# Local and global attention with an MLP on one core: the weights' lower parts move to VectorE, the loads get one fixed order with one more place, and zero products are put ahead of some of TensorE's first work

## The chip, the cores and the metric

The kernel runs on one core of a Trainium2 chip. Five engines work side by side: TensorE (PE, matrix products; its weight loads are listed as PEld), VectorE (DVE), ScalarE (ACT), GpSimd (POOL) and SyncE (SP), whose queue issues nearly all transfers. The metric is the device time of one execution in microseconds (us).

## The reference

Eight batches with eight heads of 64 are computed. 32 global queries see all 544 keys (32 global and 512 local); 512 local queries see the 32 global keys and those local keys that are at most 32 positions away. The attention's output, 4352 rows of 512 numbers, goes through x @ w_in, SiLU and @ w_out with 2048 hidden units, all in float32.

```python
s_ll = np.where(np.abs(pos[:, None] - pos[None, :]) <= window, s_ll, -1e9)
s_l  = np.concatenate([scale * q_l @ k_g.T, s_ll], axis=-1)
x    = np.concatenate([softmax(s_g) @ v_all, softmax(s_l) @ v_all], axis=2)
h    = x @ w_in
out  = (h * (1 / (1 + np.exp(-h)))) @ w_out
```

## The kernel before

**Stages and tiles.** Local attention is cut into stages: one for each batch b, each 128 local queries c and each pair of heads pr, 128 stages k in all. A stage is `st_load` (queries and keys, one DMA), `st_scores` (two products into a PSUM bank s; DVE adds the mask and takes the minimum in one instruction, L345; ACT takes the exponential, L349; DVE forms the reciprocals; ACT scales one half, L353, and DVE the other, L354), `st_turn` (four PE transposes by the identity, L382, copied back by ACT, L384) and `st_out` (eight small products with the values into a bank o, L413; ACT rounds them to xh, L420; DVE subtracts to get the rest xl, L421). Values are loaded by `st_vload`: one stage at a time for the first four, then four stages in one DMA. The global queries of a batch have four steps for pairs of heads: `g_load`, `g_scores` (L250, copied by ACT, L251), two softmaxes over 544 columns (`g_soft`, L270 to L275) and two groups of transposes (`g_turn`, L288 and L291). Global work of batch 0 lies among the first stages.

**The MLP.** Three output tiles of 128 rows (two at the end) make a block. For each block and each of 16 slices f of the hidden units, `first_layer` does 12 products of 384 columns (L568), ACT and DVE form the SiLU in two parts, gh (L577) and gl (L578), and `second_layer` adds three products for each tile (L590 to L592). All products use rounded numbers and the rest apart: high by high, high by rest, rest by high. After a product group `fill` calls `advance`, which emits the next attention steps, so attention for the next block is spread over the MLP of this one. Ahead of block 0 there is no MLP to spread it over: all twelve stages of that block stand there alone.

**The weights** arrive as 64-bit words. `fetch_weights` loads half a slice; `join_weights` makes float32 of it (ACT L203, DVE L205 and L206); `split_weights` rounds it with ACT (L215), and POOL subtracts the rounded part to get `w_lo` (L216). Six halves are joined and two slices split ahead of the MLP, the rest during its first block.

**What sets the order.** PE's order is the program's. Each step has a due time (`FIRST` for the first four stages, `DUE` and others later), all steps are sorted by it, and emitted in that order. On the other engines and on SP a planner that simulates the program chooses the order, except for instructions in `hold(...)`, which keep the program's order among themselves. The weights' instructions are held; the loads of stages from 28 on are held by `steady`; the first 28 stages' loads are left to the planner.

**Places.** `raw_tile` gives the early loads four places in turn: two of the pool `raws`, and two tiles that later hold rounded weights (`wh14`, `wh15`). A load into a place that is in use waits on SP for the products that read it, and every later load waits behind it. Early, banks of the MLP serve as extra banks for attention (`attbank`).

**At the start** POOL makes the identity, three masks, and clears the four whole tiles for probabilities, in an order that the planner chooses.

Of the kernel before, what the change touches and what calls it, by code (L numbers as in the profile page):

```python
# [9 lines left out]
F32 = mybir.dt.float32  # L10
F32R = mybir.dt.float32r
BF16 = mybir.dt.bfloat16
# [4 lines left out]
ALU = mybir.AluOpType  # L17
# [4 lines left out]
P = 128  # L22
NC = SL // P
NPR = H // 2
NST = NC * NPR
W = 224
# [15 lines left out]
KF = 24  # L42
GF = 3
KP = 12
SINGLE = 12
SCRATCH = 8
FETCH, LOOK = 6, 3
FIRSTW = {2: 1, 3: 1, 4: 1, 5: 1, 6: 1, 7: 1, 8: 1, 9: 1, 10: 1, 11: 1}
JOINS, SPLITS = (9.0, 9.6, 10.2, 10.8, 11.4, 12.0), (12.1, 12.7)

FIRST = dict(load=(-1.2, -1.1, -1.0, 0.1), vload=(-0.9, 0.2, 0.3, 1.1), turn=(3.2, 4.0, 4.9, 5.8), out=(4.3, 5.2, 6.1, 7.0),
             gload=(1.2, 2.2, 3.2, 3.3), gscores=(3.4, 4.2, 5.1, 6.0), gsoft=(4.4, 6.2), gturn=(6.9, 8.0),
             late=8.5, then=7.3)

DUE = dict(load=-1.2, split=-0.5, turn=1.6, out=2.2)
# [10 lines left out]
def attention_moe_kernel(ctx: ExitStack, tc: tile.TileContext, qk0_in, qk_in, v_in, gqk, wts, out):  # L66
# [25 lines left out]
        return ps_att.tile([P, 512], F32, tag=f"att{kind}", name=name)  # L92


    id32 = work.tile([P, P], F32R, tag="qk", bufs=BUFS["qk"], name="id32").bitcast(F32)
    make_identity(nc, id32)
    ident = const.tile([P, P], F32R, name="ident")
    nc.vector.tensor_copy(out=ident, in_=id32)

    masks = []  # L100
    for kind in range(3):
        m = const.tile([P, W], BF16, name=f"mask{kind}")
        nc.gpsimd.memset(m, 0.0)
        band = m[:, : W - SG]
        nc.gpsimd.affine_select(out=band, in_=band, pattern=[[1, W - SG]], compare_op=ALU.is_ge,
                                fill=NEG, base=0, channel_multiplier=-1)
        nc.gpsimd.affine_select(out=band, in_=band, pattern=[[-1, W - SG]], compare_op=ALU.is_ge,
                                fill=NEG, base=2 * HALO, channel_multiplier=1)
        if kind == 0:
            nc.gpsimd.memset(m[:, :HALO], NEG)  # L110
        if kind == 2:
            nc.gpsimd.memset(m[:, W - SG - HALO : W - SG], NEG)
        masks.append(m)
    mask_of = [masks[0]] + [masks[1]] * (NC - 2) + [masks[2]]


    taken = set()

    def scratch(i, dtype, name):
        return const.tile([P, 2 * DM], dtype, tag=f"wh{i}", name=name)  # L120
# [4 lines left out]
    probs += [more[:, DM * i : DM * (i + 1)].rearrange("p (u j) -> p u j", u=2) for i in range(2)]  # L125
    vfirst = scratch(7, F32, "vfirst")
    vsecond = scratch(5, F32, "vsecond")
    for t in probs:
        nc.gpsimd.memset(t, 0.0)
    pgs = [const.tile([P, SKV], F32, name=f"pg{i}") for i in range(2)]  # L130

    pts = [const.tile([P, 2, 2, P + SG], F32, name=f"pt{i}") for i in range(BUFS["pt"])]
# [16 lines left out]
    homes = itertools.count()  # L149

    def raw_tile(name, whole=False):
        i = next(homes) % 4 if whole else 0
        if i % 2 and 14 + i // 2 not in taken:
            return scratch(14 + i // 2, F32, name)
        return raws.tile([P, QW + KW], F32, tag="raw", name=name)
# [5 lines left out]


    w_32, w_hi, w_lo, w_raw, w_next = [], [], [], [], [0, 0]

    hold = tc.keep_in_program_order

    def steady(k, load):
        if k >= ND:
            hold(load)

    def fetch_weights():
        i = w_next[0]
# [36 lines left out]
    def split_weights(f):  # L209
        w_hi.append(const.tile([P, 2 * DM], F32R, tag=f"wh{f}", name=f"w_hi{f}"))  # L210
        w_lo.append(const.tile([P, 2 * DM], F32R, tag=f"ws{f}", name=f"w_lo{f}"))
        for c0 in range(0, 2 * DM, DM):
            sl = slice(c0, c0 + DM)
            hi, lo, w = w_hi[f][:, sl], w_lo[f][:, sl], w_32[2 * f + c0 // DM]
            hold(nc.scalar.copy(out=hi, in_=w))  # L215
            hold(nc.gpsimd.tensor_tensor(out=lo, in0=w, in1=hi.bitcast(F32), op=ALU.subtract))  # L216


    state = {}

    def g_load(b, p):
        raw = raw_tile(f"raw_g{b}_{p}", b < GF)
        steady(b * NST - 4, nc.sync.dma_start(out=raw[:, :GW], in_=gqk[b, p]))
        state["graw", p] = raw

    def g_split(b, p):
# [50 lines left out]
    def g_turn(b, hh):  # L277
        did(("turn", b, hh), ("soft", b, hh), ("turn", b, 0) if hh else ("last", b - 1))
        if hh == 0:

            state["pgt"] = (work.tile([P, NC, H, SG], F32, tag="pgt", name=f"pgt{b}"),
                            work.tile([P, QG], F32, tag="pgu", name=f"pgu{b}"))
        pgt, pgu = state["pgt"]
        hs = slice(4 * hh, 4 * hh + 4)
        tb = attbank("t", f"gt{b}_{hh}")
        for i in range(4):
            sl = slice(i * P, (i + 1) * P)
            nc.tensor.transpose(tb[:, sl], pgs[hh][:, sl], ident.bitcast(F32))  # L288
        nc.scalar.copy(out=pgt[:, :, hs, :], in_=tb.rearrange("p (t h q) -> p t h q", t=4, h=4))
        tb = attbank("s", f"gu{b}_{hh}")  # L290
        nc.tensor.transpose(tb[:SG, :P], pgs[hh][:, 4 * P :], ident.bitcast(F32))  # L291
        for i in range(2):
            rows, src = slice(SG * (2 * hh + i), SG * (2 * hh + i + 1)), tb[:SG, QG * i : QG * (i + 1)]
            nc.scalar.copy(out=pgu[rows, :], in_=src)
# [4 lines left out]
    def st_load(k, b, c, pr):  # L299
        raw = raw_tile(f"raw{k}", k < ND)  # L300
        if k < ND:
            nc.sync.dma_start(out=raw[:, : QW + W], in_=qk0_in[k])
        else:
            steady(k, nc.sync.dma_start(out=raw, in_=qk_in[k - ND]))
        tiles["raw", k] = raw

    def st_vload(k, b, c, pr):
        n = NPR - pr if k >= NPR else 1
        if k < 2 * NPR:
            vraw = (vfirst, vsecond)[k // NPR][:, VW * pr : VW * (pr + n)]  # L310
        else:
            vraw = raws.tile([P, NPR * VW], F32, tag="vraw", bufs=1, name=f"vraw{k}")
        vraw = vraw.rearrange("p (n w) -> p n w", n=n)
        steady(k, nc.sync.dma_start(out=vraw, in_=v_in[b, c, pr : pr + n].rearrange("n p w -> p n w")))
        for i in range(n):
            tiles["vraw", k + i] = vraw[:, i].rearrange("p (a u d) -> p a u d", a=2, u=2)

# [10 lines left out]
    def st_scores(k, b, c, pr):  # L328
        if k < ND:
            raw = tiles.pop(("raw", k))  # L330
        else:
            qk, klo = tiles.pop(("qk", k))
        s = attbank("s", f"s{k}")
        ss = [s[:, u * W : (u + 1) * W] for u in range(2)]
        for u in range(2):
            qs, ks = slice(u * P, (u + 1) * P), slice(u * W, (u + 1) * W)
            if k < ND:
                nc.tensor.matmul(ss[u], raw[:, qs], raw[:, QW : QW + W], start=True, stop=True)
            else:
                nc.tensor.matmul(ss[u], qk[:, qs], qk[:, QW:][:, ks], start=True, stop=False)  # L340
                nc.tensor.matmul(ss[u], qk[:, qs], klo[:, ks], start=False, stop=True)  # L341
        p = probs_tile(k)
        st = small.tile([P, 8], F32, tag="st", name=f"st{k}")
        for u in range(2):
            nc.vector.tensor_tensor_reduce(out=p[:, u, :W], in0=ss[u], in1=mask_of[c],  # L345
                                           scale=-SCALE, scalar=3.0e38, op0=ALU.add, op1=ALU.min,
                                           accum_out=st[:, u : u + 1])
        for u in range(2):
            nc.scalar.activation(p[:, u, :W], p[:, u, :W], AF.Exp, bias=st[:, u : u + 1], scale=-1.0,  # L349
                                 accum_out=st[:, 2 + u : 3 + u])  # L350
        nc.vector.tensor_scalar(out=st[:, 4:6], in0=st[:, 2:4], scalar1=1e-9, scalar2=None, op0=ALU.add)
        nc.vector.reciprocal(out=st[:, 6:8], in_=st[:, 4:6])  # L352
        nc.scalar.activation(p[:, 0, :W], p[:, 0, :W], AF.Copy, scale=st[:, 6:7])  # L353
        nc.vector.tensor_scalar(out=p[:, 1, :W], in0=p[:, 1, :W], scalar1=st[:, 7:8], scalar2=None,  # L354
                                op0=ALU.mult)
        tiles["p", k] = p.rearrange("p u j -> p (u j)")
# [39 lines left out]
    def st_out(k0, n, b, c, t):  # L396
# [5 lines left out]
        for j in range(n):  # L402
            k = k0 + j
            vraw, pt = tiles.pop(("vraw", k)), tiles.pop(("pt", k))
            if k < NPR:
                tiles["late", k] = vraw
            if j % 2 == 0:
                banks_.append(attbank("o", f"o{k}"))
            o = banks_[-1][:, wide * (j % 2) : wide * (j % 2 + 1)]
            for a in range(2):  # L410
                m = wide if (a == 0 or c == NC - 1) and k >= NPR else P
                for u in range(2):
                    nc.tensor.matmul(o[D * u : D * (u + 1), :m], vraw[:, a, u, :], pt[:, u, a, :m], start=(a == 0),  # L413
                                     stop=(a == 1))
# [279 lines left out]
```

## Time and profile before

| | |
|---|---|
| median of 3 runs (lowest to highest) | 1004.57 us (1003.56 to 1006.97) |
| the profiled execution | 1005.77 us, of which the span of instructions is 1004.0 |
| PE busy | 968.4 us (96%) |
| DVE, ACT, POOL busy | 619.7, 580.9, 225.6 us |
| mean granted clock of PE | 0.988 |
| moved by DMA | 151.03 MB |

Stretches are given in microseconds from the start of the span. In the view of stretches each engine has its busy time and, in brackets, its instructions; then come PE's granted clock (1.00 is full), the share of the 16 transfer engines' time that was busy, and GB/s. In the view in order of time a row has start, length, engine, line, operation, output <- input, and in square brackets the idle time of the engine before it with what ended it. In the groups a row ends in busy time and mean ns of one, then the idle time before them. A row of waits has the total, the count and the longest. Matmuls overlap, so the length of one is more than its distance to the next.

### The profile page before, as it was taken

To read this page: it belongs to the slowest core of one execution; us is meant where nothing else is said; L and a number is where in the kernel's file an instruction comes from. 1 tells how busy PE (TensorE), PEld (TensorE's weight loads), DVE (VectorE), ACT (ScalarE), POOL (GpSimd) and SP (SyncE) were. 2 spreads that over 40 slices of the span, in tenths; PEclk is the share of its full clock that TensorE was granted. 3 is DMA by queue.
4 is the path that set the end of the run, shared out by engine and by line. 5 is a ranking of instruction groups with operands and counts; after the bars stand their busy time and mean duration, and the time that the engine had idled before them with its cause. 6 is when DMAs were issued, how large, how long until landed. Compare 5 with 4: busy or idle time off the path is not lost.

```text
span 1004.0 us, 17484 instructions
## 1 busy us (share of the span) xinstructions
PE 968.4 (96%) x5792; PEld 854.7 (85%) x5792; DVE 619.7 (62%) x1861; ACT 580.9 (58%) x1491; POOL 225.6 (22%) x421
## 2 busy tenths in 40 slices
PE   6888899999899999999999999999999999999998
PEld 4567778889798989998899989998998989889896
DVE  3678885566577567755576666775677665553332
ACT  5787765566566656654466656665666655443332
POOL 2144433222122221211222121222222221211000
PEclk8899999999999999999999999999999999999999
DMA  8574544656666656645476466565666555333000
GB/s 295 189 254 146 153 129 140 165 135 167 197 158 172 176 161 178 160 118 138 106 193 178 119 194 188 163 176 142 176 179 185 139 151 165 106 100 84 2 22 22
DMA packets 175626, 151.03 MB, mean 150 GB/s; under 512 B 115888, under 2 KB 135856, under 8 KB 175536
## 3 DMA queue, kind: packets, MB, share of 16 engines
q1 hardware_dynamic: 171312, 142.31, 50.8%
q10 hardware_dynamic: 4224, 7.60, 2.1%
q8 instruction: 46, 0.75, 0.3%
q14 instruction: 44, 0.36, 0.1%
HBM read 86.44 MB, written 36.18 MB: 122 GB/s over the span
## 4 chain that ended last, share of the span: by engine, by line
PE 78%; DMA 2%; DVE 2%; issue 2%; ACT 1%; POOL 0%; SPq 0%; POOLq 0%; DVEq 0%; ACTq 0%
PE h L568 33%; PE out L592 11%; PE out L590 11%; PE out L591 11%; PE o L413 6%; PE s L340 2%; PE s L341 2%; DMA raw<-in_qk_dram 1%; DMA raw_g<-in_gqk_dram 1%; PE gt L288 1%; DMA away<-halves 0%; PE gs L254 0%; PE gs L253 0%; DVE gl L578 0%; DVE w L206 0%
## 5 line engine op out<-in xcount | busy, mean ns | idle before, releaser
L568 PE MATMUL h<-xh,w_lo 128*128 128x384 f32 (+1 forms) x768 | 252.2, 328 | 2.8 <-POOL w_lo L216 2.8
L568 PE MATMUL h<-xh,w_hi 128*128 128x384 f32 (+1 forms) x768 | 253.4, 330 | 0.7 <-ACT w_hi L215 0.7
L568 PE MATMUL h<-xl,w_hi 128*128 128x384 f32 (+1 forms) x768 | 251.4, 327 | 0.3 <-DVE xl L421 0.3
L364 POOL COPY halves<-probs 128x512 uint16<-128x512 uint16 x208 | 135.0, 674 | 437.9 <-DVE probs L354 203.1
L590 PE MATMUL out<-w_hi,gh 128*128 128x512 f32 x544 | 221.1, 406 | 5.6 <-ACT gh L577 5.5
L592 PE MATMUL out<-w_hi,gl 128*128 128x512 f32 x544 | 216.5, 398 | 5.5 <-DVE gl L578 5.2
L591 PE MATMUL out<-w_lo,gh 128*128 128x512 f32 x544 | 214.1, 394 | 0.0
L574 ACT ACTIVATE t<-h 128x384 f32<-128x384 f32 (+1 forms) x192 | 90.6, 472 | 178.7 <-PE h L568 160.2
L575 DVE SCALAR_TENSOR_TENSOR t<-t,h 128x384 f32<-128x384 f32 (+1 forms) x192 | 101.7, 530 | 108.6 <-ACT t L574 107.5
L349 ACT ACTIVATE probs<-probs,st 128x224 f32<-128x224 f32 x244 | 115.8, 475 | 64.8 <-DVE st L345 63.8
L568 PEld LDWEIGHTS h<-xh,w_hi 128*128 128x128 f32 x768 | 145.0, 189 | 8.7 <-ACT w_hi L215 1.5
L568 PEld LDWEIGHTS h<-xl,w_hi 128*128 128x128 f32 x768 | 145.0, 189 | 7.1 <-DVE xl L421 0.6
L568 PEld LDWEIGHTS h<-xh,w_lo 128*128 128x128 f32 x768 | 144.7, 188 | 3.7 <-POOL w_lo L216 3.7
L578 DVE TENSOR_TENSOR gl<-t,gh 128x384 fp32r<-128x384 f32 (+1 forms) x192 | 107.4, 559 | 57.7 <-PE out L592 43.8
L592 PEld LDWEIGHTS out<-w_hi,gl 128*128 128x128 f32 x544 | 102.4, 188 | 35.6 <-DVE gl L578 13.4
L577 ACT CAST gh<-t 128x384 fp32r<-128x384 f32 (+1 forms) x192 | 94.5, 492 | 58.6 <-DVE t L575 58.0
L345 DVE CUSTOM_DVE_ANT_0 probs<-s,mask 128x224 f32<-128x224 f32 x244 | 85.7, 387 | 68.0 <-PE s L341 54.0
L590 PEld LDWEIGHTS out<-w_hi,gh 128*128 128x128 f32 x544 | 102.8, 189 | 27.3 <-ACT gh L577 11.0
L591 PEld LDWEIGHTS out<-w_lo,gh 128*128 128x128 f32 x544 | 102.9, 189 | 12.8
L324 ACT CAST qk<-raw 128x704 fp32r<-128x704 f32 x100 | 77.6, 776 | 31.9 <-DMA raw<-in_qk_dram 24.4
L325 DVE TENSOR_TENSOR klo<-raw,qk 128x448 fp32r<-128x448 f32 x100 | 64.8, 648 | 41.3 <-ACT qk L324 39.7
L353 ACT ACTIVATE probs<-probs,st 128x224 f32<-128x224 f32 x122 | 58.7, 481 | 33.5 <-DVE st L352 30.3
(86 smaller groups left out, 1122.3 us busy)
## 6 DMA issues: line engine op xcount, KB each, us to landing
raw<-in_qk_dram SPq DMA_DIRECT2D x100, 352.0 KB, 3.4
away<-halves SPq DMA_DIRECT2D x104, 256.0 KB, 2.6
vraw<-in_v_dram SPq DMA_DIRECT2D x30, 512.0 KB, 4.6
raw_w<-in_wts_dram SPq DMA_DIRECT2D x24, 512.0 KB, 4.6
raw_g<-in_gqk_dram SPq DMA_DIRECT2D x32, 304.0 KB, 4.0
out_dram<-o ACTq DMA_DIRECT2D x28, 256.0 KB, 3.6
raw<-in_qk_dram SPq DMA_DIRECT2D x28, 240.0 KB, 2.8
raw_w<-in_wts_dram SPq DMA_DIRECT2D x16, 256.0 KB, 3.3
```

What stands on the lines that cost most here:

```text
L324: nc.scalar.copy(out=qk, in_=raw)
L345: nc.vector.tensor_tensor_reduce(out=p[:, u, :W], in0=ss[u], in1=mask_of[c], scale=-SCALE, scalar=3.0e38, op0=ALU.add, op1=ALU.min, accum_ ...
L349: nc.scalar.activation(p[:, u, :W], p[:, u, :W], AF.Exp, bias=st[:, u : u + 1], scale=-1.0, accum_out=st[:, 2 + u : 3 + u])
L364: nc.gpsimd.tensor_copy(out=halves[:, :, u], in_=p[:, 2 * P * u : 2 * P * (u + 1)].bitcast(U16).rearrange("p (j h) -> p h j", h=2))
L568: nc.tensor.matmul(h[:, :nt], wt, x[:, c, :nt], start=(i == 0), stop=(i == 3 * NCC - 1))
L574: nc.scalar.activation(t[:, :nt], h[:, :nt], AF.Tanh, scale=0.5)
L575: nc.vector.scalar_tensor_tensor(out=t[:, :nt], in0=t[:, :nt], scalar=1.0, in1=h[:, :nt], op0=ALU.add, op1=ALU.mult)
L577: nc.scalar.copy(out=gh[:, :nt], in_=t[:, :nt])
L578: nc.vector.tensor_tensor(out=gl[:, :nt], in0=t[:, :nt], in1=gh[:, :nt].bitcast(F32), op=ALU.subtract)
L590: nc.tensor.matmul(o, gh[:, sl], wh, start=(f == 0), stop=False)
L591: nc.tensor.matmul(o, gh[:, sl], wl, start=False, stop=False)
L592: nc.tensor.matmul(o, gl[:, sl], wh, start=False, stop=(f == NF - 1))
```

## The change

Five things are changed.

1. `split_weights` subtracts on VectorE instead of GpSimd.
2. All loads are held: `g_load`, `st_load` and `st_vload` keep the program's order on SP together with the weights. In `FIRST` the first value loads move from −0.9, 0.2, 0.3 and 1.1 to 1.22, 1.23, 2.22 and 2.23; the global loads move from 1.2, 2.2, 3.2 and 3.3 to 1.2, 1.21, 2.2 and 2.21. The ten early weight loads, one each with stages 2 to 11, go two each with stages 4 and 5 and one each with 6 to 11.
3. The fifth early load gets a place of its own (`wh13`); the ring of four goes on behind it.
4. Products of a zero tile (bf16, 288 columns) are issued on PE into columns that the next group overwrites: 14 ahead of the first scores, 8 ahead of the second group of global transposes of batch 0, and 3 ahead of each o of stages 4 to 11.
5. POOL's first work is held in a new order: the first mask, then only the pads of the probability tiles (32 columns of each half), then the identity, then the other masks.

```diff
+WARM = 288
+WARMS = (14, 8, 3)
-FIRSTW = {2: 1, 3: 1, 4: 1, 5: 1, 6: 1, 7: 1, 8: 1, 9: 1, 10: 1, 11: 1}
+FIRSTW = {4: 2, 5: 2, 6: 1, 7: 1, 8: 1, 9: 1, 10: 1, 11: 1}
-FIRST = dict(load=(-1.2, -1.1, -1.0, 0.1), vload=(-0.9, 0.2, 0.3, 1.1), turn=(3.2, 4.0, 4.9, 5.8), out=(4.3, 5.2, 6.1, 7.0),
-             gload=(1.2, 2.2, 3.2, 3.3), gscores=(3.4, 4.2, 5.1, 6.0), gsoft=(4.4, 6.2), gturn=(6.9, 8.0),
+FIRST = dict(load=(-1.2, -1.1, -1.0, 0.1), vload=(1.22, 1.23, 2.22, 2.23), turn=(3.2, 4.0, 4.9, 5.8), out=(4.3, 5.2, 6.1, 7.0),
+             gload=(1.2, 1.21, 2.2, 2.21), gscores=(3.4, 4.2, 5.1, 6.0), gsoft=(4.4, 6.2), gturn=(6.9, 8.0),
...
+    zeros = two.tile([P, WARM], BF16, tag="gl", bufs=1, name="zeros")
+    nc.vector.memset(zeros, 0.0)
+
+    def warm(bank, n):
+        for _ in range(n):
+            nc.tensor.matmul(bank[:, 512 - WARM :], zeros[:, :P], zeros, start=True, stop=True)
...
-    for t in probs:
-        nc.gpsimd.memset(t, 0.0)
+    def pads():
+        for t in probs:
+            hold(nc.gpsimd.memset(t[:, :, W:], 0.0))
...
-        i = next(homes) % 4 if whole else 0
+        i = next(homes) if whole else 0
+        if whole and i == NPR:
+            return scratch(13, F32, name)
+        i = (i - (i > NPR)) % 4
...
-    def steady(k, load):
-        if k >= ND:
-            hold(load)
...
-            hold(nc.gpsimd.tensor_tensor(out=lo, in0=w, in1=hi.bitcast(F32), op=ALU.subtract))
+            hold(nc.vector.tensor_tensor(out=lo, in0=w, in1=hi.bitcast(F32), op=ALU.subtract))
...
-        steady(b * NST - 4, nc.sync.dma_start(out=raw[:, :GW], in_=gqk[b, p]))
+        hold(nc.sync.dma_start(out=raw[:, :GW], in_=gqk[b, p]))
...
+        if b == 0 and hh:
+            warm(tb, WARMS[1])
...
-            nc.sync.dma_start(out=raw[:, : QW + W], in_=qk0_in[k])
+            hold(nc.sync.dma_start(out=raw[:, : QW + W], in_=qk0_in[k]))
...
-        steady(k, nc.sync.dma_start(out=vraw, in_=v_in[b, c, pr : pr + n].rearrange("n p w -> p n w")))
+        hold(nc.sync.dma_start(out=vraw, in_=v_in[b, c, pr : pr + n].rearrange("n p w -> p n w")))
...
+        if k == 0:
+            warm(s, WARMS[0])
...
+                if NPR <= k < SINGLE:
+                    warm(banks_[-1], WARMS[2])
```

More of the change, by code (lines that the diff above doesn't have):

```diff
@@ L92, in attbank @@
         return ps_att.tile([P, 512], F32, tag=f"att{kind}", name=name)
[L95 to L114, printed above, removed]
+    hold = tc.keep_in_program_order
+    zeros = two.tile([P, WARM], BF16, tag="gl", bufs=1, name="zeros")
[3 more added lines that the diff above has]
+            nc.tensor.matmul(bank[:, 512 - WARM :], zeros[:, :P], zeros, start=True, stop=True)
     taken = set()
@@ L127, in attention_moe_kernel @@
     vsecond = scratch(5, F32, "vsecond")
-    for t in probs:
-        nc.gpsimd.memset(t, 0.0)
+    def pads():
+        for t in probs:
+            hold(nc.gpsimd.memset(t[:, :, W:], 0.0))
+    masks = []
+    for kind in range(3):
+        m = const.tile([P, W], BF16, name=f"mask{kind}")
+        hold(nc.gpsimd.memset(m, 0.0))
+        band = m[:, : W - SG]
+        hold(nc.gpsimd.affine_select(out=band, in_=band, pattern=[[1, W - SG]], compare_op=ALU.is_ge,
+                                     fill=NEG, base=0, channel_multiplier=-1))
+        hold(nc.gpsimd.affine_select(out=band, in_=band, pattern=[[-1, W - SG]], compare_op=ALU.is_ge,
+                                     fill=NEG, base=2 * HALO, channel_multiplier=1))
+        if kind == 0:
+            hold(nc.gpsimd.memset(m[:, :HALO], NEG))
+            pads()
+            id32 = work.tile([P, P], F32R, tag="qk", bufs=BUFS["qk"], name="id32").bitcast(F32)
+            make_identity(nc, id32)
+            ident = const.tile([P, P], F32R, name="ident")
+            nc.vector.tensor_copy(out=ident, in_=id32)
+        if kind == 2:
+            hold(nc.gpsimd.memset(m[:, W - SG - HALO : W - SG], NEG))
+        masks.append(m)
+    mask_of = [masks[0]] + [masks[1]] * (NC - 2) + [masks[2]]
     pgs = [const.tile([P, SKV], F32, name=f"pg{i}") for i in range(2)]
@@ L163, in attention_moe_kernel @@
     w_32, w_hi, w_lo, w_raw, w_next = [], [], [], [], [0, 0]
-    hold = tc.keep_in_program_order
-    def steady(k, load):
-        if k >= ND:
-            hold(load)
     def fetch_weights():
@@ L301, in st_load @@
         if k < ND:
-            nc.sync.dma_start(out=raw[:, : QW + W], in_=qk0_in[k])
+            hold(nc.sync.dma_start(out=raw[:, : QW + W], in_=qk0_in[k]))
         else:
-            steady(k, nc.sync.dma_start(out=raw, in_=qk_in[k - ND]))
+            hold(nc.sync.dma_start(out=raw, in_=qk_in[k - ND]))
         tiles["raw", k] = raw
```

## The prediction

> **What bounds the kernel now.** I read the busy times by stretch first, cut where the work of TensorE (PE) changes: loads and first scores, the first global queries, the rest of attention ahead of the MLP, the first MLP pass, and everything after it.
>
> ```profile
> core 0: us, PE busy (x) PEld busy (x) DVE busy (x) ACT busy (x) POOL busy (x), PEclk, DMA share, GB/s
> 0.00:11.67 11.67, 7.75 (x28) 5.93 (x28) 5.16 (x29) 6.74 (x22) 5.55 (x25) 1.00 0.82 253
> 11.67:24.71 13.04, 9.36 (x57) 6.06 (x57) 3.16 (x10) 7.04 (x19) 0.00 (x0) 0.74 0.93 331
> 24.71:28.08 3.37, 1.60 (x12) 1.27 (x10) 2.14 (x11) 2.66 (x11) 0.80 (x4) 1.00 0.80 274
> 28.08:35.11 7.03, 7.03 (x39) 5.45 (x37) 2.66 (x13) 3.59 (x12) 0.98 (x5) 0.51 0.34 113
> 35.11:55.15 20.04, 16.56 (x122) 12.10 (x121) 15.54 (x68) 19.06 (x58) 5.09 (x11) 1.00 0.66 216
> 55.15:150.00 94.85, 84.51 (x459) 69.97 (x457) 78.80 (x193) 68.75 (x175) 38.97 (x36) 0.98 0.53 168
> 150.00:1004.00 854.00, 841.64 (x5087) 753.95 (x5085) 512.23 (x1538) 473.01 (x1201) 174.20 (x344) 1.00 0.52 143
> ```
>
> From 150 us on PE works 841.64 of 854.00 us at full clock. The loads of that stretch keep their order among the steps, all but the last few subtractions of weights lie before it, and there is no filler in it: I carry it over unchanged. Everything is decided in the first 150 us, and since PE sets the rest, a microsecond won there is a microsecond at the end. Each of the first six stretches has another limit. Next I read PE's instructions in order of time, for the waits in brackets.
>
> ```profile
> 3.36 5.38 PE L338 MATMUL s<-raw 128*128 128x224 f32 x16 [3.36 <-DMA raw<-in_qk_dram]
> ...
> 11.04 0.63 PE L382 MATMUL t<-ident,probs 128*128 128x128 f32 x4 [0.50 <-ACT probs L353]
> 13.57 0.90 PE L250 MATMUL gs<-raw_g 128*64 128x272 f32 x3 [1.90 <-DMA raw_g<-in_gqk_dram]
> ...
> 18.50 1.62 PE L250 MATMUL gs<-raw_g 128*64 128x272 f32 x3 [1.78 <-DMA raw_g<-in_gqk_dram]
> ...
> 24.72 1.02 PE L338 MATMUL s<-raw 128*128 128x224 f32 x4
> 27.50 0.63 PE L288 MATMUL gt<-ident,pg 128*128 128x128 f32 x4 [1.76 <-DVE st L351]
> ...
> 42.91 0.66 PE L382 MATMUL t<-ident,probs 128*128 128x128 f32 x4 [1.07 <-ACT probs L353]
> ```
>
> Between 11.67 and 24.71 PE stops twice for global queries that have not landed, and the clock falls. The loads in the order of SP's queue, and the landing times of the global queries, say why:
>
> ```profile
> 7.13 0.65 SPq L185 DMA_DIRECT2D raw_w<-in_wts_dram  x1
> 7.82 0.73 SPq L314 DMA_DIRECT2D vraw<-in_v_dram  x1
> 8.60 0.69 SPq L185 DMA_DIRECT2D raw_w<-in_wts_dram  x1
> 9.38 1.06 SPq L223 DMA_DIRECT2D raw_g<-in_gqk_dram  x2
> ```
>
> ```profile
> DMA to landing us min/median/max: 2.7/4.5/9.2
> ```
>
> The third global load is issued at 9.38 and used at 18.50: those 9.1 us are the maximum of 9.2. Ahead of it stand weights and values that nobody reads before o and the MLP; the transfer engines are 93% busy, so it is a queue and not a latency. The last limit is in the first MLP pass, 55.15 to 150, where PE is idle for 10.3 of 94.85 us. Its waits:
>
> ```profile
> PE out L590 <- ACT gh L577: 3.3, 4, 1.6
> PE out L592 <- DVE gl L578: 3.1, 3, 2.4
> PE h L568 <- POOL w_lo L216: 2.8, 3, 1.1
> ```
>
> **The loads.** Eight rows of SP's issues change places. The four small value loads leave their places among the first scores' loads, the global loads come right behind these, and the weights and the large values stand behind the stage loads for k=4 and 5. Ahead of the last global load there are then, by their shapes, four stage loads (128 x 480 f32, 240 KB each), three global ones (128 x 608, 304 KB) and two values (128 x 256, 128 KB), about 2.1 MB. Before, the stage loads, four values, two global loads, three weights, vsecond and vraw (128 x 1024, 512 KB each of the last five) made 4.6 MB. The extra place lets the first global load go without a wait. The second now waits on SP for the scores of stage 0 (free at about 6 us), and behind it stand the values of stages 0 and 1 and the other global loads; o of stage 0 would wait for them. With the median landing of 4.5 us they are there at 10 to 12 us, which is when PE reaches gs and o (gs at best at 11.67). So both DMA waits go. What is late next is ACT: its 7.04 us of work between 11.67 and 24.71. PE's own work there is 9.36, but a mean clock of 0.74 over 13.04 us is 6.8 us at half clock, of which 1.8 were the second wait; 5.0 busy us at half speed become 2.5, leaving 6.9. The stretch can thus fall from 13.04 to 7.0 and no lower. PE and ACT hand tiles to each other stage by stage and neither fills 7 of 7; I take 8.5, **a gain of 4.5**, with 2 (a new wait on ACT chains as long as half of the old ones) and 6 as ends. The weights start some 7 us later than now; their first reader is at 40.4 us, so that is hidden by about 25 us:
>
> ```profile
> L205 DVE TENSOR_SCALAR raw_w<-raw_w x40: 282/422/1526, 40.4 to 149.8; 128x512 uint32<-128x512 uint32 x24, 128x256 uint32<-128x256 uint32 x16
> L206 DVE SCALAR_TENSOR_TENSOR w<-w,raw_w x40: 411/693/1578, 41.6 to 151.3; 128x512 uint32<-128x512 uint32 x24, 128x256 uint32<-128x256 uint32 x16
> ```
>
> Without that cover each weight piece would cost 512 KB at 331 GB/s, 1.5 us.
>
> **The zero products.** No row shows a bf16 product. The nearest are fp32r products of 384 columns, which start 0.17 us apart at full clock:
>
> ```profile
> 56.01 0.33 PE L568 MATMUL h<-xl,w_hi 128*128 128x384 f32 x1
> 56.18 0.33 PE L568 MATMUL h<-xh,w_lo 128*128 128x384 f32 x1
> ```
>
> 288 columns are then 0.13 us, or 0.26 at half clock; as the lower end I take nothing at all (a filler that lies wholly in a wait). The first 14 take 3.6 us cold. They begin at about 1 us, when the zeros are written, and end near 4.7, so they hold up the first scores by 1.3 us (these start at 3.36 now). That is hidden: the first reduction waits for a mask until 5.74.
>
> ```profile
> 5.74 0.39 DVE L345 CUSTOM_DVE_ANT_0 probs<-s,mask 128x224 f32<-128x224 f32 x1 [3.94 <-POOL mask L110]
> ```
>
> The mask comes first in POOL's new order, so without the fillers DVE would start near 4.3 (3.36 and two cold products); with them at about 5.5. The 1.3 us are lost out of what the mask gives. In return the clock is up sooner: the scores run 581 ns each at first and 352 later, which the clock column (1.00) doesn't show there.
>
> ```profile
> L338 PE MATMUL s<-raw x4: 581/581/581, 5.8 to 6.9; 128*128 128x224 f32 x4
> L338 PE MATMUL s<-raw x4: 352/352/353, 7.8 to 8.4; 128*128 128x224 f32 x4
> ```
>
> Stage 3's scores end near 7.9 instead of 8.74, but ACT is the limit there; **0.3** for the start (−1.3 to +1.0). The eight at the second transpose of the global softmax, 1.0 us, lie in the wait of 1.76: nothing. What they are worth is the clock after it:
>
> ```profile
> 14.00:15.00 1.00, 1.00 (x10) 0.72 (x8) 0.00 (x0) 0.52 (x2) 0.00 (x0) 0.73 1.11 392
> ...
> 28.00:29.00 1.00, 1.00 (x6) 0.93 (x4) 0.03 (x1) 0.95 (x3) 0.12 (x1) 0.55 0.00 0
> ```
>
> Waits of 1.90 and 1.76 us were each followed by a half clock, the one of 1.07 at 42.91 was not (the clock of 35.11 to 55.15 is 1.00). A filled gap leaves less than 1 us. Then the stretch from 28.08, PE busy throughout at clock 0.51, falls from 7.03 to 3.5 us of PE, or 3.59 of ACT; with the hand-overs 4.5, **a gain of 2.5** (0 to 3.4). The Trainium skill ("TensorE: Matmul & The Clock Gate", Part 1) says the clock halves only after about one idle window of 3.4 us. This trace differs: no gap after the first loads reached 2 us. By that rule the gap of 1.76 would not have cooled and these 2.5 would not be there to win; the rows decide.
>
> The last 24, three ahead of each o of stages 4 to 11, are 3.1 us of PE in a region where ACT is busy 19.06 of 20.04 us and PE idles 3.5. They go into waits, or move the next tile by less than the wait that follows: **a loss of 0.5** (0 to 3.1). If ACT stopped being the limit the whole 3.1 would show.
>
> **The subtraction on VectorE.** First DVE and POOL by shape from 50 to 155 us, then two of DVE's shapes between 200 and 800, where POOL subtracts nothing:
>
> ```profile
> L206 DVE SCALAR_TENSOR_TENSOR w<-w,raw_w 128x512 uint32<-128x512 uint32 x20 | 15.6, 778 | 4.1 <-ACT w L203 3.2
> L205 DVE TENSOR_SCALAR raw_w<-raw_w 128x512 uint32<-128x512 uint32 x20 | 12.8, 641 | 0.0
> L205 DVE TENSOR_SCALAR raw_w<-raw_w 128x256 uint32<-128x256 uint32 x16 | 12.2, 764 | 0.0
> L206 DVE SCALAR_TENSOR_TENSOR w<-w,raw_w 128x256 uint32<-128x256 uint32 x16 | 11.8, 737 | 1.0
> L578 DVE TENSOR_TENSOR gl<-t,gh 128x384 fp32r<-128x384 f32 x14 | 9.7, 693 | 4.7 <-ACT gh L577 4.4 <-PE out L592 0.3
> ```
>
> ```profile
> L216 POOL TENSOR_TENSOR w_lo<-w,w_hi 128x512 fp32r<-128x512 f32 x32 | 45.0, 1428 | 52.1 <-DVE raw_w L205 26.5 <-ACT w_hi L215 18.0 <-issue 4.2
> ```
>
> ```profile
> L578 DVE TENSOR_TENSOR gl<-t,gh 128x384 fp32r<-128x384 f32 x117 | 66.7, 570 | 22.4 <-PE out L592 17.4 <-ACT gh L577 4.1 <-PE h L568 0.3
> L233 DVE TENSOR_TENSOR klo_g<-raw_g,qk_g 128x544 fp32r<-128x544 f32 x20 | 14.5, 725 | 6.2 <-ACT qk_g L232 6.0
> ```
>
> The nearest row for the new operation is L233 (725 ns for 544 columns): 0.68 us for 512, 32 of them 21.8 us. On POOL one took 1.43. DVE is busy 78.80 of 94.85 us, so 21.8 more would not fit. But half-width shifts average 764 ns where the undisturbed one takes 282, longer than full-width ones: they lose time to something. Taking the minimum and median of L205 (282 and 422) and of L206 (411 and 693) and 570 for L578 as undisturbed, the excess is 4.4 + 7.7 + 1.7 + 5.2 + 1.7 = 20.7 us. I take all of it for POOL's subtractions, so DVE's load grows by 1.1 only. PE's waits for w_lo (2.8) go, as it is ready some 0.7 us sooner per half; of the 6.4 for gh and gl half goes, because no DVE instruction lasts 1.5 us any more; new ones come, since the subtraction waits on DVE for ACT's rounding, and behind it stand L575 and L578, on which ACT's gh and PE's second layer wait: I allow 2.5. **Gain 3.5** (9.2 if every such wait goes; −6 if none goes and DVE's excess stays in part).
>
> **The sum**: 4.5 + 0.3 + 2.5 − 0.5 + 3.5 = 10.3 us. The profiled execution took 1005.77 (span 1004.0), so 995.5 for one like it; the median of the runs, 1004.57, is 1.2 below that execution: **994.3**.
>
> **Rivals.** (1) *The hand-over between PE and ACT takes the place of the DMA waits*, with gaps of over 1.7 us and a half clock again: the loads give 2, the clock stretch 0.5, the start and the fillers −0.2, the MLP 3.5: 998.8. For it speaks ACT's 7.04 us of work; against it that no wait on ACT ahead of the MLP exceeds 1.08 now. (2) *DVE becomes the bound of the first MLP pass*: the long rows are not POOL's doing, or only half. Then DVE gets 21.8 − 10.4 = 11.4 us more, with the same idle time, and the pass grows by that: 1004.57 − 6.8 + 11.4 = 1009.2. It is slower from the point where less than about 15 of the 20.7 us come back. Against it stands that L578 takes 693 here and 570 elsewhere, and for it the order on one engine, which strings ACT's rounding and DVE's products together. The Trainium skill ("GPSIMD Engine Reference", Key points) has GpSimd share its SBUF interfaces with VectorE, in contention with two-input and two-port instructions; by that all of it comes back, and this rival falls. (3) *Zero products don't hold the clock*: PE is busy with them but the clock stays half. The first scores then start at 4.7 and run 5.9 us, ending 2 later; the 2.5 are not won: 1004.57 − (4.5 − 2 − 0.5 + 3.5) = 999.1. (4) *The pinned loads block each other on SP*: a stage load behind a weight load that waits for its place costs PE in the MLP what the global loads give, 4.5, and the 3.5 there aren't won: 1004.57 − 10.3 + 8.0 = 1002.3. For it speaks that the stage loads had no fixed place among the weights so far; against it that no row here shows PE waiting for one after 3.36 us.
>
> **How the numbers follow.** Chances: the forecast 0.59, (1) 0.18, (2) 0.08, (3) 0.08, (4) 0.07. The lower end of the range takes 6 for the loads, 3.4 for the clock and 8 for the MLP, with the 0.3 and the −0.5: 987.4; the upper end holds (1) and (3) and stops short of (4): 1001.5. About 0.3%, 3 us, can be told from no change. The forecast, (1) and (3) are faster, 0.84 with a little off for the worse ends of (1); (4) is the same, 0.08; (2) is slower, 0.08.
>
> **What would show it.** The first gs of each pair no longer waits for raw_g, and scores of stage 4 start near 20 us instead of 24.72. The clock from then to the MLP is 1.00. The first layer starts at 46 to 49 us, not 55.15. L205 and L206 sit at 0.28 to 0.69 us, DVE's busy time in the first pass is about what it was, and that pass takes 90 to 92 us instead of 94.85. DVE busy over 90% in that pass, or new waits of PE for raw, would make the forecast wrong.

## The result and the profile after

The changed kernel takes 1019.93 us (median of four, 1018.50 to 1022.89) against 1005.22 for the kernel before (which has a fourth execution by now): a ratio of 1.0137, 95% interval 1.0106 to 1.0168. It was forecast at 994.3 and faster; it is slower, and outside the range. The profiled execution took 1019.24 us with a span of 1017.4.

The same cuts as before the change, moved to where the same instructions stand now; only the last cut, at 163, lies where the loss has ended. The view is that of busy times by stretch: length, PE, PEld, DVE, ACT, POOL, the granted clock, the share of the transfer engines, GB/s.

```profile
core 0: us, PE busy (x) PEld busy (x) DVE busy (x) ACT busy (x) POOL busy (x), PEclk, DMA share, GB/s
0.00:11.36 11.36, 8.78 (x43) 6.12 (x44) 5.22 (x30) 6.92 (x23) 4.13 (x25) 1.00 0.79 235
11.36:18.23 6.87, 6.87 (x57) 4.71 (x58) 2.87 (x10) 6.32 (x19) 0.00 (x0) 1.00 0.98 317
18.23:21.63 3.40, 2.57 (x19) 2.04 (x18) 2.38 (x11) 2.60 (x10) 0.80 (x4) 1.00 0.98 298
21.63:25.89 4.26, 4.26 (x41) 3.42 (x40) 2.67 (x14) 3.57 (x12) 0.87 (x5) 1.00 1.05 392
25.89:47.09 21.20, 19.22 (x143) 13.70 (x142) 18.32 (x75) 20.58 (x62) 1.94 (x8) 1.00 0.85 298
47.09:163.00 115.91, 88.96 (x446) 75.98 (x445) 73.27 (x212) 67.37 (x170) 3.08 (x8) 0.88 0.41 131
163.00:1017.40 854.40, 842.95 (x5100) 755.25 (x5098) 514.55 (x1545) 473.28 (x1203) 169.74 (x340) 1.00 0.53 143
```

The reader is to see two things. Up to the first layer of the MLP the signs that were forecast are there: it starts at 47.09 us instead of 55.15, at full clock, with PE busy throughout two of the stretches. From 163 us on hardly anything has changed (854.40 us for 5100 products, 854.00 for 5087 before). The whole loss lies in the first MLP pass, which has 27 idle microseconds of PE and a clock of 0.88. PE's waits over the whole run (total, times, longest):

```profile
PE s L352 <- DMA raw<-in_qk_dram: 22.6, 6, 6.2
PE h L584 <- DVE w_lo L226: 3.5, 3, 2.6
PE out L608 <- DVE gl L594: 2.5, 6, 0.6
...
PE out L606 <- ACT gh L593: 1.6, 3, 0.7
```

The waits for gh, gl and w_lo were 9.2 us in the first pass before; of the rows above only 3.5 us for w_lo and 0.7 for gh lie in that pass now. New are 22.6 us for stage loads, all in it. The first of these, one from the middle and the longest, in PE's order of time, and then SP's queue over part of the same time:

```profile
69.28 1.83 PE L352 MATMUL s<-raw 128*128 128x224 f32 x4 [3.10 <-DMA raw<-in_qk_dram]
...
100.96 1.83 PE L352 MATMUL s<-raw 128*128 128x224 f32 x4 [4.42 <-DMA raw<-in_qk_dram]
...
149.83 1.83 PE L352 MATMUL s<-raw 128*128 128x224 f32 x4 [6.25 <-DMA raw<-in_qk_dram]
```

```profile
45.81 16.93 SPq L195 DMA_DIRECT2D raw_w<-in_wts_dram  x2
62.79 0.43 SPq L326 DMA_DIRECT2D vraw<-in_v_dram  x1
63.27 0.49 SPq L314 DMA_DIRECT2D raw<-in_qk_dram  x1
...
73.58 22.64 SPq L195 DMA_DIRECT2D raw_w<-in_wts_dram  x3
96.32 0.38 SPq L314 DMA_DIRECT2D raw<-in_qk_dram  x1
```

A merged row lasts from its first issue to the end of its last. From 73.58 to 96.22 three weight loads occupy the queue; the stage load behind them goes out at 96.32 and its scores start at 100.96, after 4.42 us in which PE had nothing to do. What the queue waits for is DVE above all:

```profile
SPq L195 <- DVE raw_w L215: 47.3, 4, 20.9
SPq L195 <- DVE w L216: 15.2, 8, 7.4
SPq L195 <- PE gs L260: 12.6, 1, 12.6
```

The 20.9 us end when DVE does its first half-width shifts, this one and one at 94.64:

```profile
93.90 0.29 DVE L215 TENSOR_SCALAR raw_w<-raw_w 128x256 uint32<-128x256 uint32 x1
```

The code gives the rest. The 12.6 us come first, in the row of 45.81: half 13 of the weights lands in `wh14`, a place of the ring, and waits for the product of a global query there; PE's stop at 69.28 is behind it. The longer waits come later. At slice f the program first joins the weight halves up to 2(f+3) and then fetches those up to 2(f+6). From slice 8 on the second half of a slice lands in one of two alternating sets of places, so half 21 needs the place of half 17. Half 21 is fetched at slice 5, as the last of the three loads at 73.58; half 17, whose two parts are the first half-width shifts, is joined at slice 6. The stage loads traced in between stand behind a wait that ends one slice later. PE meanwhile needs them, so PE stops, so ACT and DVE get to the join later still.

How could the kernel before do this without harm? The text ahead of the prediction says that held instructions keep the program's order among themselves. The order of SP's instructions shows that it is less: a held one stands behind the instruction traced just before it on its engine, and if that one is not held itself, the two may drift together. In the kernel before, the second half of slice 6 (half 13) was issued behind half 19, and a stage load went between:

```
SP, kernel before, in order (half of the weights in brackets)
raw_w (12), vraw, raw, raw_w (14), raw, raw_w (18), raw_w (19, two parts), raw_w (13), raw, raw_w (20), ...
SP, changed kernel
raw_w (12), raw_w (13), vraw, raw, raw_w (14), raw_w (15), raw_w (16), raw_w (17, two parts), raw, raw_w (18),
raw_w (19, two parts), raw, raw_w (20), raw_w (21, two parts), raw, ...
```

With every load held there is one fixed chain, and the planner can no longer put a load that has its place ahead of one that has not.

### The profile page after: what moved, and what is told of

The parts are those of the page before. It is cut to its first block, busy times and chain, and to the rows that moved or that the text cites. A ratio compares the mean times of both kernels' runs of the same rounds, so it can differ in the third digit from the quotient of the medians.

```text
span 1017.4 us, 17554 instructions
## 1 busy us (share of the span) xinstructions
PE 973.6 (96%) x5838; PEld 861.2 (85%) x5838; DVE 619.3 (61%) x1894; ACT 580.6 (57%) x1491; POOL 180.6 (18%) x389
## 4 chain that ended last, share of the span: by engine, by line
PE 78%; DMA 10%; DVE 6%; ACT 3%; issue 1%; SPq 1%; POOL 0%; ACTq 0%; DVEq 0%; POOLq 0%
PE h L584 31%; PE out L606 11%; PE out L608 11%; PE out L607 10%; DMA raw<-in_qk_dram 6%; PE o L429 6%; DMA away<-halves 2%; PE s L352 2%; PE s L354 2%; PE s L355 2%; DMA raw_g<-in_gqk_dram 1%; DVE w L216 1%; PE t L396 1%; PE gs L260 1%; ACT qk L336 1%
```

## The experiments

Two theories stood against each other. **A**: a weight load that waits on SP for its place holds up the stage loads pinned behind it. **B**: VectorE, with the subtractions in its order, is the bound of the first pass. "First layer" is the start of its first product, "pass" the time from there to the first store of output, both from the view in order of time of the profiled execution; medians are of all runs. Ratios and intervals are to runs of the kernel before on the same chip, whose median went from 1004.9 to 1008.1 us between the sets.

| | median us | ratio to before, interval | first layer | pass | wait for raw after the first layer starts |
|---|---|---|---|---|---|
| before | 1005.22 | 1 | 55.15 | 113.1 | 0 |
| changed | 1019.93 | 1.0137 (1.0106 to 1.0168) | 47.09 | 136.5 | 22.6 |
| pinned up to the MLP only | 989.41 | 0.9837 (0.9799 to 0.9874) | 48.13 | 102.6 | 0 |
| the same, subtraction on GpSimd | 998.59 | 0.9936 (0.9916 to 0.9956) | 47.51 | 114.2 | 0 |
| all pinned, subtraction on GpSimd | 1020.96 | 1.0154 (1.0119 to 1.0190) | 47.08 | 138.7 | 27.3 |
| all pinned, fetch five ahead | 988.50 | 0.9828 (0.9786 to 0.9871) | 47.19 | 104.9 | 0.7 |

### Pinned up to the MLP only

```diff
+    def steady(k, load):
+        if early or k >= ND:
+            hold(load)
...
-            hold(nc.sync.dma_start(out=raw[:, : QW + W], in_=qk0_in[k]))
+            steady(k, nc.sync.dma_start(out=raw[:, : QW + W], in_=qk0_in[k]))
```

(and the same for `g_load` and `st_vload`; `early` is emptied when the first layer begins)

> The changed kernel, with its loads pinned only up to the start of the MLP; the stage loads of the first MLP pass are left to the planner again, as before the change. Theory A (a weight load that waits on SP for its place holds up the stage loads pinned behind it): TensorE's 22.6 us of waits for raw vanish, its clock stays full, the first MLP pass takes 88 to 96 us instead of 116, the median is 992 to 998 us. Theory B (VectorE, with the subtractions in its order, is the bound of that pass): the waits move to DVE, the pass stays over 108 us and the median over 1010.

989.41 us, under the range that theory A gave; the pass is 33.9 us shorter than in the changed kernel, where 20 to 28 were expected (the 116 us of the expectation count to the cut at 163, the table to the first store). The wait for raw is not in the view of PE's waits any more; these are its largest rows:

```profile
PE out L610 <- ACT gh L597: 4.1, 6, 1.6
PE out L612 <- DVE gl L598: 3.0, 6, 1.2
```

```profile
47.10:138.00 90.90, 86.81 (x494) 74.43 (x491) 79.56 (x228) 72.79 (x186) 3.79 (x9) 1.00 0.56 174
```

The clock is 1.00 in the pass, and VectorE is busy 79.56 of 90.90 us (88%) without stopping PE for more than 1.2 us by gl. Theory B falls. Pinning the loads of the first pass costs 1019.93 − 989.41 = 30.5 us. What it is made of shows in the pass up to the first store, which has 566 products in both kernels; first the changed kernel, then this one:

```profile
47.09:183.54 136.45, 109.50 (x566) 93.00 (x565) 85.31 (x247) 79.78 (x200) 6.73 (x17) 0.90 0.40 125
48.13:150.69 102.56, 98.47 (x566) 84.25 (x565) 84.59 (x247) 78.45 (x200) 6.97 (x16) 1.00 0.53 166
```

PE is idle for 26.95 us against 4.09, and busy for 109.50 against 98.47 with the same products. So 22.9 of the 33.9 us by which the pass is longer are idle time, which is the 22.6 of waits for raw, and 11.0 go with the lower clock, 0.90 against 1.00. (Ahead of the pass and behind it the changed kernel is some 3.7 us quicker in these two executions.)

### The subtraction, with the first pass free and pinned

```diff
-            hold(nc.vector.tensor_tensor(out=lo, in0=w, in1=hi.bitcast(F32), op=ALU.subtract))
+            hold(nc.gpsimd.tensor_tensor(out=lo, in0=w, in1=hi.bitcast(F32), op=ALU.subtract))
```

> As the run with loads pinned only up to the MLP, and the subtraction back on GpSimd. Theory A with the forecast's 3.5 us for the move to VectorE: 2 to 6 us slower than that run, the shifts and ors of VectorE stretched to 1.5 us again. Theory B: faster than that run by over 10 us.

998.59: with the first pass free, the subtraction on VectorE is worth 9.2 us, more than the 2 to 6 us that were expected under theory A. DVE by shape, from 45 to 155 us, with the subtraction on GpSimd:

```profile
L219 DVE TENSOR_SCALAR raw_w<-raw_w 128x256 uint32<-128x256 uint32 x16 | 12.2, 764 | 0.0
L220 DVE SCALAR_TENSOR_TENSOR w<-w,raw_w 128x256 uint32<-128x256 uint32 x16 | 11.9, 741 | 1.0
L598 DVE TENSOR_TENSOR gl<-t,gh 128x384 fp32r<-128x384 f32 x15 | 11.4, 762 | 6.2 <-ACT gh L597 4.4 <-PE out L612 1.8
```

and, over the same time, with the subtraction on VectorE (the kernel pinned up to the MLP only):

```profile
L230 DVE TENSOR_TENSOR w_lo<-w,w_hi 128x512 fp32r<-128x512 f32 x31 | 20.2, 690 | 0.2 <-ACT w_hi L229 0.2
...
L598 DVE TENSOR_TENSOR gl<-t,gh 128x384 fp32r<-128x384 f32 x17 | 9.4, 555 | 4.9 <-ACT gh L597 3.6 <-PE out L612 1.2
...
L220 DVE SCALAR_TENSOR_TENSOR w<-w,raw_w 128x256 uint32<-128x256 uint32 x16 | 6.8, 424 | 1.0
L219 DVE TENSOR_SCALAR raw_w<-raw_w 128x256 uint32<-128x256 uint32 x16 | 4.7, 292 | 0.0
```

The half-width shift takes 764 ns on average beside GpSimd's subtraction and 292 without, the half-width or 741 and 424, gl 762 and 555. The edit between the two changes nothing but the engine of the subtraction, so the long rows are GpSimd's doing. The kernel with the subtraction on GpSimd, over the stretch of time that was quoted for the other:

```profile
47.10:138.00 90.90, 81.99 (x442) 69.14 (x442) 74.66 (x178) 64.38 (x162) 37.95 (x35) 0.96 0.54 169
```

PE is busy 81.99 us at a clock of 0.96 in these 90.90 us, against 86.81 at 1.00: 4.8 us more of idle time, and by the mean clock about 3.6 us of lost speed.

> The changed kernel with only the subtraction put back on GpSimd, all loads pinned. Theory A: TensorE still waits some 20 us for raw, median 1017 to 1026. Theory B: the raw waits go, median under 1003.

1020.96, as theory A has it. With all loads pinned the engine of the subtraction makes no difference that can be told (1019.93 and 1020.96): DVE's time is not what PE waits for there.

### All pinned, the fetch one slice later

```diff
-FETCH, LOOK = 6, 3
+FETCH, LOOK = 5, 3
```

> The changed kernel, all loads pinned, but in the first MLP pass a weight is fetched five slices ahead instead of six, so that the place it needs has been freed by a join that stands earlier in the program. Theory A: SP's waits ahead of weight loads shrink from 47 us (for the shift of a join) to under 15, TensorE's waits for raw fall under 8 us, median 993 to 1003. If pinning itself is at fault, whatever the places: raw waits stay near 20 us, median over 1013.

988.50, under the range that was given: one number undoes the loss, with the pins left in. Half 21 is now fetched at slice 6, behind the join that frees its place. But one part of the expectation missed. Instead of under 15 us, SP still waits 26.8 for the shifts of joins, and more for other places:

```profile
SPq L195 <- DVE raw_w L215: 26.8, 4, 13.5
SPq L195 <- PE gs L260: 13.8, 1, 13.8
SPq L195 <- DVE w L216: 11.9, 8, 4.8
```

These are 52.5 us against 75.1, while PE's waits for raw went from 22.6 to 1.0. So the time that a queue waits is no measure of the harm. What counts is which load stands behind the wait:

```profile
46.80 0.43 SPq L326 DMA_DIRECT2D vraw<-in_v_dram  x1
47.54 0.33 SPq L314 DMA_DIRECT2D raw<-in_qk_dram  x1
47.98 15.80 SPq L195 DMA_DIRECT2D raw_w<-in_wts_dram  x4
63.82 0.43 SPq L314 DMA_DIRECT2D raw<-in_qk_dram  x1
```

The long wait is there, with 15.80 us, but the values and the stage load that stood behind it in the changed kernel (62.79 and 63.27) are now ahead of it. The load of 47.54 is the one whose product runs at 66.13 us; in the changed kernel it went out at 63.27 for the product that stopped at 69.28.

### The fillers

```diff
-WARMS = (14, 8, 3)
+WARMS = (0, 0, 0)
```

Left out here are only products of zeros; the kernel computes the same.

> The changed kernel with the fetch five slices ahead (988.5 us) without any zero products. If the fillers are worth the clock they hold, as forecast (2.5 + 0.3 - 0.5): 989.5 to 993 us, with a half clock somewhere between 17 and 35 us. If the early global loads alone keep the clock up, the fillers only cost: 986 to 988.5, clock 1.00 from 10 us on.

990.71 (ratio 0.9854, 0.9816 to 0.9891), beside 988.50 (0.9828, 0.9786 to 0.9871) with the fillers: not told apart, though 990.71 lies in the first range. The sign of that range, a half clock between 17 and 35 us, is missing. Without fillers:

```profile
18.00:22.00 4.00, 2.12 (x18) 1.42 (x17) 2.60 (x13) 3.09 (x11) 0.80 (x4) 1.00 0.99 320
22.00:26.00 4.00, 4.00 (x36) 3.39 (x38) 2.50 (x12) 3.33 (x10) 0.86 (x4) 1.00 1.06 395
```

PE idles 1.9 us in the first of these stretches, in one wait ahead of the second global transposes, and the clock is 1.00 after it. The first layer starts at 46.54 us, 0.65 ahead of the kernel with fillers, which is no more than two executions of that kernel differ by (47.19 and 47.85, below).

### The old due times, pinned

```diff
-FIRSTW = {4: 2, 5: 2, 6: 1, ...}     vload=(1.22, 1.23, 2.22, 2.23)     gload=(1.2, 1.21, 2.2, 2.21)
+FIRSTW = {2: 1, 3: 1, 4: 1, 5: 1, 6: 1, ...}     vload=(-0.9, 0.2, 0.3, 1.1)     gload=(1.2, 2.2, 3.2, 3.3)
```

> The changed kernel with the fetch five slices ahead (988.5 us), but the due times of the first values, of the first global loads and of the early weights as before the change; all loads stay pinned, in that order. If the order of these loads is what brings the first layer from 55 to 47 us, TensorE waits for raw_g again, the first layer starts at 50 to 55, median 991 to 997. If the extra place, the mask and the fillers bring it, the median stays at 987 to 990.

991.34 (0.9864, 0.9825 to 0.9904), inside the first range by 0.3 us, but its signs are missing: PE waits 0.2 us for raw_g, and the first layer starts at 47.94, not at 50 to 55. The interval overlaps with that of 988.50. What the due times are worth once the order is the program's can't be told from nothing here.

### One part at a time from the kernel before

The subtraction alone (the one line above, from GpSimd to VectorE):

> The kernel before with only the subtraction moved to VectorE. Forecast for this part 3.5 us (1001); from the pair of runs with and without it behind the early gains it is 9.2 us (about 996). VectorE's shifts and ors stand at 0.28 to 0.69 us, the first layer still starts near 55 us. If it were the bound of the pass: over 1008.

994.17 (0.9892, 0.9858 to 0.9927): 11 us. The first layer starts at 51.22 rather than near 55, which was not expected. Ahead of the MLP the loads stand in the same order on SP as in the kernel before, PE's order is the program's in both, and the waits for raw_g are still there (3.4 us). What differs is the clock: it is half for 3.4 us, from 14.24 on, where the kernel before had it half for 13.7, from 14.46 to 21.28 and from 28.11 to 34.94. So about 4 us of this execution's gain lie ahead of the MLP and come with the clock, and 8.2 lie in the pass (104.9 against 113.1 us). Whether the edit has a part in the former is not shown.

The pins alone:

```diff
-        if k >= ND:
-            hold(load)
+        hold(load)
...
-            nc.sync.dma_start(out=raw[:, : QW + W], in_=qk0_in[k])
+            hold(nc.sync.dma_start(out=raw[:, : QW + W], in_=qk0_in[k]))
```

> The kernel before with only its loads all pinned in the program's order (old due times, old ring, fetch six ahead, subtraction on GpSimd). Theory A: the blocked queue alone makes the loss, TensorE waits 15 to 30 us for raw in the first MLP pass, median 1015 to 1035. If the blocking comes from the ring's new place (the weight that waited 12.6 us for a global query's place): raw waits under 8 us, median 1003 to 1010.

1020.52 (1.0156, 1.0117 to 1.0196). Its waits:

```profile
PE s L337 <- DMA raw<-in_qk_dram: 28.3, 7, 8.2
```

The blocked queue alone makes the loss, in the old ring too (3.5 of the 28.3 us are the first load, which every kernel without fillers waits for). And the first layer starts at 46.88 us with old due times, no fillers, no new place and the old order on GpSimd.

### The parts that are left

The last four ran side by side on one chip. The first has `if early or k >= ND` in `steady` and the stage loads under it, with the subtraction on VectorE; the second has these pins with the subtraction left on GpSimd; the third pins all loads, with the fetch five ahead and the subtraction on VectorE; the fourth is the changed kernel with the fetch five ahead once more.

> The kernel before with two edits only: the subtraction on VectorE, and the loads pinned up to the start of the MLP (old due times, old ring, no fillers, old order on GpSimd). If the pinned order and the subtraction carry the whole gain: 986 to 991, equal to the changed kernel with the fetch five slices ahead. If fillers, place, mask and the new due times carry a part: 992 to 997.

> The kernel before with one edit: the loads pinned up to the start of the MLP. If the order ahead of the MLP is worth what the first layer's start shows (47 us against 55): 995 to 999, no waits for raw_g, the first layer at 46 to 49 us. If the planner's order costs nothing there: 1003 to 1006.

> The kernel before with the subtraction on VectorE, all loads pinned, and the fetch five slices ahead; nothing else. If the fetch distance alone turns the pinning of the first MLP pass from a loss into none, also in the old ring: 986 to 992, waits for raw under 6 us. If it needs the ring's new place: over 998.

> The changed kernel with the fetch five slices ahead once more, beside the three smaller versions on the same chip: 986 to 991. A difference to the first or third of over 3 us is the worth of fillers, place, mask and due times together; under that it can't be told from nothing.

| | median us | ratio to before, interval | first layer |
|---|---|---|---|
| pins up to the MLP, subtraction on VectorE | 989.16 | 0.9818 (0.9791 to 0.9845) | 47.10 |
| pins up to the MLP alone | 999.22 | 0.9918 (0.9885 to 0.9950) | 46.78 |
| all pinned, fetch five ahead, subtraction on VectorE | 988.84 | 0.9821 (0.9789 to 0.9853) | 46.38 |
| the whole change, fetch five ahead | 989.70 | 0.9819 (0.9791 to 0.9848) | 47.85 |

Two edits give as much as the whole change with its loss mended: 989.16 and 989.70. Fillers, extra place, masks and due times together can't be told from nothing, where 3 us could have been. The order ahead of the MLP is worth 0.8% (0.8 us of waiting for raw_g is left, where none was expected), the subtraction on VectorE another 10.1 us (999.22 − 989.16). With these pins alone the clock is full where the kernel before had it half:

```profile
22.00:26.00 4.00, 3.81 (x33) 3.24 (x33) 2.53 (x13) 3.04 (x10) 0.88 (x4) 1.00 0.96 324
```

## Why the prediction was wrong

**The stage loads of the first pass were priced at nothing: this step failed.** The sum followed the eight rows of SP that move ahead of the MLP, and said of the pins only what they do there. What the pins do to the 16 later stage loads among the weights was left to rival (4), at 0.07 and with a price of 4.5 us plus 3.5 not won. The mechanism of that rival is the one that came; its price is 30.5 us. The row that was held against that rival (no PE wait for a stage load after 3.36 us) spoke of a queue in which the planner was free to reorder, which is what the change takes away. The place could have been found from the code: half 21 needs the place of half 17, and is fetched one slice ahead of that join. With the loads pinned up to the MLP only, and so without this step, the kernel takes 989.41 us, inside the range of the forecast.

**The loads ahead of the MLP: 4.5 forecast.** The stretch from the end of the second transposes to the scores of stage 4 went from 13.04 to 6.87 us: 6.2, past the end of 6 that was given. The hand-overs between PE and ACT cost less than was allowed. But the reason was wrong in part. The new due times are not needed for it: the old ones do as well once they are kept. The planner had put three weights and the large values ahead of the third global load; with the old due times pinned, two weights and no large values stand there.

**The clock: 2.5 forecast.** The stretch from 28.08 went from 7.03 to 4.26 us, 2.8. That the size fits is luck, for its cause was given as the eight fillers, and they are not needed: without any, the clock is 1.00 there as well. The reading that gaps of 1.76 us cool and gaps of 1.07 don't was too simple: the wait at the second global transposes is 1.76 us again in the kernel with the subtraction alone, and the clock stays at 1.00.

```profile
26.63 0.63 PE L288 MATMUL gt<-ident,pg 128*128 128x128 f32 x4 [1.76 <-DVE st L351]
```

The Trainium skill ("TensorE: Matmul & The Clock Gate", Part 1) describes a window of 3413 ns that runs freely and does not start anew with the kernel. The traces agree with a grid of that step: the clock of the kernel before is half from 14.46 to 21.28 and from 28.11 to 34.94 us, two steps of 3.41 each time. But where the gap falls on the grid does not settle this case. It lies within one step in both kernels; here are that step and the next, first in the kernel before, then with the subtraction alone:

```profile
24.70:28.11 3.41, 1.65 (x12) 1.30 (x11) 2.14 (x11) 2.70 (x11) 0.80 (x4) 1.00 0.79 272
28.11:31.53 3.42, 3.42 (x23) 2.74 (x21) 0.71 (x4) 2.08 (x8) 0.87 (x4) 0.50 0.22 45
...
24.48:27.90 3.42, 1.66 (x12) 1.20 (x10) 2.14 (x11) 2.74 (x9) 0.23 (x1) 1.00 0.70 252
27.90:31.31 3.41, 3.40 (x35) 2.72 (x34) 2.65 (x13) 2.73 (x9) 1.02 (x5) 1.00 0.51 125
```

PE is busy 1.65 us of the step in one and 1.66 in the other, and half a step of idling was enough once and not the other time. What decided stays open.

**The start: 0.3 forecast**, and the second transposes end 0.3 us earlier (11.36 against 11.67). The 14 fillers ran from 1.07 to 4.37 and DVE's first reduction began at 5.29 us instead of 5.74. Rival (3) falls with them: zero products do bring up the clock, as the scores behind them take 3.33 us for what took 5.38.

```profile
1.07 3.30 PE L103 MATMUL s<-zeros 128*128 128x288 bf16 x14 [1.07 <-DVE zeros L99]
4.21 3.33 PE L352 MATMUL s<-raw 128*128 128x224 f32 x16
```

It is worth nothing here: the first transposes, which wait for ACT, start at 9.13 us with fillers and at 9.11 without (both with the fetch five ahead).

**The fillers of stages 4 to 11: a loss of 0.5 forecast.** The stretch grew from 20.04 to 21.20, 1.2; leaving all fillers out moved the first layer by 0.65, within what two executions of one kernel differ by. The sign is the one that was given; the loss can't be told from nothing in the medians. All parts together, 0.3 + 6.2 + 2.8 − 1.2, are the 8.1 us by which the first layer comes sooner; 6.8 was forecast.

**The subtraction: 3.5 forecast, 9.2 to 11 measured.** 0.68 us a piece was right (0.690), and so was it that the long shifts and ors are GpSimd's doing. (In the 11 us some 4 are those of the clock ahead of the MLP.) The term was mis-sized twice. The two kernels with the pins up to the MLP, with the subtraction on GpSimd and on VectorE and no other edit, show it over the pass to the first store. Of PE's waits for gh and gl, 6.4 us, only 0.4 are left, where half was allowed; those for w_lo are 2.2 in place of 2.8, near the 2.5 that were allowed for new ones. And idle time has a second price: PE is busy 102.11 us for the 566 products with the subtraction on GpSimd, at a clock of 0.98, and 98.85 at 1.00 without. These 3.3 us no term had. Rival (2), DVE as the bound, falls: DVE is 88% busy in the free pass and PE idles 4.1 of 90.9 us. That part of the Trainium skill on which it hung ("GPSIMD Engine Reference", Key points: contention with two-input and two-port instructions of VectorE) agrees with the rows of the two-input or, 424 against 741 ns, and of gl, 555 against 762; whether the one-input shift, 292 against 764, ran in a two-port mode no row shows.

## What to carry to other kernels

To pin a queue's order is to promise that each entry can go when its turn comes. Before pinning, follow each entry that may wait for a place to the instruction that frees that place, and see whether it stands ahead of the fetch in the program; if not, everything pinned behind inherits the wait, and a fetch that reaches less far can be faster. A queue's total waiting says little: 52 us did no harm here and 75 cost 30, for the difference lay in what stood behind. And when a change has several parts, run them apart: here the subtraction and the fixed order ahead of the MLP carried the gain, what the others did can't be told from nothing, and the loss came from the pins, which also brought a gain.

## What was not expected of the hardware

- A subtraction on GpSimd stretches VectorE's half-width shift from 292 to 764 ns on average. Moving the work to the busier engine shortened the whole by 9 to 11 us, and VectorE's busy time over the whole run did not grow: 619.7 us before, 617.4 with 32 subtractions more.
- The same idle gap of 1.76 us on TensorE is followed by a half clock in one kernel and by a full one in another, though about half of a step of 3.41 us was idle in both. The same wait, 1.70 to 1.88 us long, was followed by a full clock in all profiles of kernels without fillers, except the one of the kernel before.
- Products of zeros raise the clock: behind 14 of 288 columns, 3.3 us in all, the first scores took 352 ns each at once. Without them they took 581 ns at first and 352 only some 4 us later.
